# Two first weight loads on one issuing queue instead of two, in a gated MLP on one Trainium2 core

## Chip, cores, metric

One core of one Trainium2 chip. Times are device microseconds (us) of one execution. A run's profile has its own clock, which starts at 0 with the program's first instruction and covers 1.8 us less than the device time. Ratios are the mean time of one kernel's fast runs over that of the other's in the same rounds, so they are not quite the ratio of the medians that are quoted beside them.

## The reference

```python
B, S, D, F = 32, 32, 512, 1792          # bf16
gate = jnp.einsum("bsd,df->bsf", x, w1)
up   = jnp.einsum("bsd,df->bsf", x, w3)
h    = _silu(gate) * up
out  = jnp.einsum("bsf,fd->bsd", h, w2)
```

That is 1024 tokens of 512 features. In the kernel D is 4 row blocks (`dt`) of 128, F is 14 tiles (`fo`) of 128, and the tokens come in two blocks of 512.

## The kernel before

Only the start matters here. The loads, in the order of the program (SyncE is `nc.sync`, ScalarE `nc.scalar`; each has its own DMA queue, q1 and q10 in the profile):

```python
FK = 3
load_x(nc.sync, 0, 1)                              # x, token tile 0
load_x(nc.scalar, 1, 2)                            # x, token tile 1
load_w(nc.sync, w1_sb, w1_v, 0, FK, 0, 2)          # w1, tiles 0-2, row blocks 0-1
nc.scalar.activation(table[:], one, SIGMOID)
load_w(nc.scalar, w1_sb, w1_v, 0, FK, 2, DT)       # w1, tiles 0-2, row blocks 2-3
load_w(nc.sync, w3_sb, w3_v, 0, FK, 0, 2)
load_w(nc.sync, w3_sb, w3_v, 0, FK, 2, DT)
nc.sync.dma_start_transpose(out=xT[:, :, HB:NB], in_=x_flat[HB:NB, :])   # tokens 256-511
for c0, c1 in ((FK, 2 * FK), (2 * FK, 10), (10, FT)):
    load_w(nc.sync, w1_sb, w1_v, c0, c1)
    load_w(nc.sync, w3_sb, w3_v, c0, c1)
# ... transpose of tokens 512-1023, w2
```

The matmuls, in order. TensorE runs 6 dummy matmuls to raise its clock, turns tokens 0-255 with 8 matmuls (`pT`), and then:

```python
for dt in range(DT):
    for fo in range(FK):
        project(gates[fo], w1_sb, fo, 0, HB, [dt])      # gate, tokens 0-255: 12 matmuls
for dt in range(DT):
    for fo in range(FK):
        project(ups[fo], w3_sb, fo, 0, HB, [dt])        # up, tokens 0-255: 12 matmuls
for fo in range(FK):
    project(gates[fo], w1_sb, fo, HB, NB, range(DT), HB)  # tokens 256-511
    project(ups[fo], w3_sb, fo, HB, NB, range(DT), HB)
    swiglu(gates[fo], ups[fo], fo, 0)
# ... the other 11 tiles, the second block of tokens, the product with w2
```

So "w1's second half" (row blocks 2-3) is needed by the seventh gate matmul, and "the tokens" (256-511) by the twenty-fifth matmul after pT. From there on the order is fixed and TensorE hardly stops.

Of the kernel before, what the change touches and what calls it, by code (L numbers as in the profile page):

```python
# [10 lines left out]
def kernel(  # L11
# [8 lines left out]
    nc = tc.nc  # L20
# [10 lines left out]
    DT = D // P  # L31
# [7 lines left out]
    w1_v = w1.rearrange("(dt p) f -> p dt f", p=P)  # L39
# [14 lines left out]
    w1_sb = consts.tile([P, DT, F], bf16, name="w1_sb")  # L54
# [4 lines left out]
    FK = 3  # L59
# [4 lines left out]
    def load_w(queue, w_sb, w_v, c0, c1, d0=0, d1=DT):  # L64
        f0, f1 = c0 * P, c1 * P
        queue.dma_start(out=w_sb[:, d0:d1, f0:f1], in_=w_v[:, d0:d1, f0:f1])
# [5 lines left out]
    load_x(nc.scalar, 1, 2)  # L72
    load_w(nc.sync, w1_sb, w1_v, 0, FK, 0, 2)
    nc.scalar.activation(table[:], one, SIGMOID)  # L74
    load_w(nc.scalar, w1_sb, w1_v, 0, FK, 2, DT)
    load_w(nc.sync, w3_sb, w3_v, 0, FK, 0, 2)
    load_w(nc.sync, w3_sb, w3_v, 0, FK, 2, DT)
    nc.sync.dma_start_transpose(out=xT[:, :, HB:NB], in_=x_flat[HB:NB, :])
# [142 lines left out]
```

## Time and profile before

| | before |
|---|---|
| median of the first three runs (range) | 82.37 us (82.08 to 82.68) |
| span of the profile | 80.9 us |
| TensorE busy | 77.1 us (95%) |
| idle time of TensorE's weight loads put down to a load | 0.9 us for x, while the dummy matmuls still ran; 0.3 us for w1's first half |

A row of the chain of waits gives start, duration and what ran. In the timeline the bracket holds the idle time before a group and what ended it. "Landing" is the time from the start of an issue until the last of the DMA engines reports its part as written. SPq stands for SyncE issuing, PE for TensorE, L66 for line 66 of the kernel (the load in `load_w`), and "issue" for time in which nothing that the profile shows was waited for. A queue's line in a DMA view gives packets, MB, and the time that its packets took as a share of the time of the 16 DMA engines.

### The profile page before, as it was taken

The numbers are of one execution on the slowest core, as the hardware profiler recorded it, in microseconds if no ns is written. First come the engines' busy times: TensorE is split into PE (matmuls) and PEld (weight loads), VectorE is DVE, ScalarE is ACT, GpSimd is POOL, SyncE is SP. The second block draws the span as 40 slices with busy tenths as digits, with TensorE's granted clock in tenths as the row PEclk, the third lists the DMA queues.
The fourth block names the chain that finished last, engine by engine and source line by source line (L and its number), as shares of the span: only waits on it lengthen the run. The fifth ranks groups of instructions, "written<-read, shape, count | busy, mean of one in ns | idle before, by whom it ended". The sixth has DMA issues, their size and how long they took to land.

```text
span 80.9 us, 1014 instructions
## 1 busy us (share of the span) xinstructions
PE 77.1 (95%) x382; PEld 37.9 (47%) x388; DVE 39.5 (49%) x60; ACT 23.4 (29%) x40; POOL 0.7 (1%) x6
## 2 busy tenths in 40 slices
PE   6999999999999999999999999999999999999960
PEld 2368854444444444444444444444444444444540
DVE  0140399898877887877878877873000000000010
ACT  4320553222343222343222443220220220220220
POOL 3000000000000000000000000000000000000000
PEclk9999999999999999999999999999999999999999
DMA  0999999999950000000000000000011011011012
GB/s 20 291 321 281 355 351 349 171 226 330 360 193 0 0 0 0 0 0 0 4 8 0 0 0 0 4 0 0 16 49 65 26 39 65 31 42 65 28 40 62
DMA packets 10789, 7.67 MB, mean 95 GB/s; under 512 B 3616, under 2 KB 10784, under 8 KB 10784
## 3 DMA queue, kind: packets, MB, share of 16 engines
q1 hardware_dynamic: 10368, 7.28, 31.2%
q10 hardware_dynamic: 416, 0.33, 1.4%
q8 instruction: 3, 0.05, 0.2%
q14 instruction: 2, 0.02, 0.1%
HBM read 5.77 MB, written 1.05 MB: 84 GB/s over the span
## 4 chain that ended last, share of the span: by engine, by line
PE 95%; issue 1%; DVE 0%; DVEq 0%
PE gate_ps L121 31%; PE o_ps L174 30%; PE up_ps L121 30%; PE warm_ps L92 3%; PE pT L104 1%; DVE o_sb L183 0%; DVEq L183 0%
## 5 line engine op out<-in xcount | busy, mean ns | idle before, releaser
L121 PEld LDWEIGHTS <-w_sb 128*128 128x128 bf16 x248 | 24.6, 100 | 24.6 <-DMA w_sb<-in_w_dram 0.3
L121 PE MATMUL gate_ps<-xT,w_sb 128*128 128x512 bf16 (+1 forms) x122 | 29.5, 368 | 0.2
L121 PE MATMUL up_ps<-xT,w_sb 128*128 128x512 bf16 (+1 forms) x122 | 28.7, 358 | 0.1
L131 ACT ACTIVATE sig<-gate_ps 128x512 f32<-128x512 f32 x28 | 16.7, 597 | 32.3 <-PE gate_ps L121 32.3
L174 PE MATMUL o_ps<-w_sb,hT 128*128 128x512 bf16 (+2 forms) x124 | 24.3, 355 | 0.1
L133 DVE TENSOR_TENSOR t<-gate_ps,sig 128x512 f32<-128x512 f32 x28 | 19.3, 690 | 9.3 <-ACT sig L131 9.2
L134 DVE TENSOR_TENSOR hT<-t,up_ps 128x512 bf16<-128x512 f32 x28 | 19.3, 688 | 2.9
L174 PEld LDWEIGHTS <-hT 128*128 128x128 bf16 x126 | 11.8, 98 | 12.7
L183 DVE CAST o_sb<-o_ps 128x128 bf16<-128x128 f32 x1 | 0.3, 292 | 23.0 <-PE o_ps L174 23.0
L185 ACT CAST o_sb<-o_ps 128x512 bf16<-128x512 f32 (+1 forms) x8 | 4.6, 572 | 19.6 <-PE o_ps L174 19.6
L92 PE MATMUL warm_ps<-const-bfloat16-1.0 128*128 128x512 bf16 x6 | 2.7, 623 | 0.8 <-PEq L205 0.8
L114 DVE CAST xT<-pT 128x256 bf16<-128x256 f32 (+1 forms) x3 | 1.1, 380 | 3.9 <-PE pT L104 3.8
L74 ACT ACT_TABLE_LOAD x1 | 1.3, 1283 | 1.2 <-PEq L205 1.2
L92 PEld LDWEIGHTS <-const-bfloat16-1.0 128*128 128x128 bf16 x6 | 0.7, 133 | 1.9 <-issue 1.9
L104 PEld LDWEIGHTS <-x_sb 128*128 128x128 bf16 x8 | 0.8, 135 | 0.9 <-DMA x_sb<-in_x_dram 0.9
L104 PE MATMUL pT<-ident,x_sb 128*128 128x128 bf16 x8 | 1.1, 308 | 0.0
L114 ACT CAST xT<-pT 128x128 bf16<-128x128 f32 (+1 forms) x2 | 0.6, 318 | 1.5 <-PE pT L104 1.5
masks.py:199 POOL TENSOR_SCALAR_AFFINE_SELECT ident<-ident 128x128 bf16<-128x128 bf16 x1 | 0.3, 292 | 0.1
masks.py:197 POOL MEMSET ident<- 128x128 bf16 x1 | 0.2, 204 | 0.3 <-POOLq L205 0.3
L74 ACT ACTIVATE table<-const-bfloat16-1.0 128x1 f32<-128x1 bf16 x1 | 0.2, 202 | 0.0
L205 POOL MEMSET const-bfloat16-1.0<- 128x1 bf16 x1 | 0.1, 102 | 0.0
L205 POOL MEMSET const-uint8-127<- 128x1 uint8 x1 | 0.1, 102 | 0.0
(2 smaller groups left out, 0.2 us busy)
## 6 DMA issues: line engine op xcount, KB each, us to landing
w_sb<-in_w_dram SPq DMA_DIRECT2D x4, 512.0 KB, 8.0
w_sb<-in_w_dram SPq DMA_DIRECT2D x1, 1792.0 KB, 8.3
out_dram<-o_sb SPq DMA_DIRECT2D x7, 128.0 KB, 1.7
w_sb<-in_w_dram SPq DMA_DIRECT2D x2, 384.0 KB, 5.7
w_sb<-in_w_dram SPq DMA_DIRECT2D x3, 192.0 KB, 3.7
w_sb<-in_w_dram ACTq DMA_DIRECT2D x1, 192.0 KB, 3.5
x_sb<-in_x_dram ACTq DMA_DIRECT2D x1, 128.0 KB, 2.9
x_sb<-in_x_dram SPq DMA_DIRECT2D x1, 128.0 KB, 2.7
```

The source lines that it names most:

```text
L74: nc.scalar.activation(table[:], one, SIGMOID)
L92: nc.tensor.matmul(warm_ps[:, 0:cols], lhsT=one.to_broadcast([P, P]), rhs=one.to_broadcast([P, cols]), start=True, stop=True,)
L104: nc.tensor.matmul(pT[:, i, j, :], lhsT=x_sb[:, nt, dt * P : (dt + 1) * P], rhs=ident[:], start=True, stop=True,)
L114: copy(xT[:, dts[0] : dts[-1] + 1, nts[0] * P : (nts[-1] + 1) * P], pT[:].rearrange("p d t c -> p d (t c)"),)
L121: nc.tensor.matmul(ps[:, c0 : c0 + n1 - n0], lhsT=w_sb[:, dt, fo * P : (fo + 1) * P], rhs=xT[:, dt, n0:n1], start=(dt == 0), stop=(dt == D ...
L131: nc.scalar.activation(sig[:], gate_ps[:], SIGMOID)
L133: nc.vector.tensor_mul(t[:], gate_ps[:], sig[:])
L134: nc.vector.tensor_mul(hT[:, fo, nb * NB : (nb + 1) * NB], t[:], up_ps[:])
L174: nc.tensor.matmul(o_ps[:], lhsT=hT[:, fo, nt * P : (nt + 1) * P], rhs=w2_sb[:, fo, c0 : c0 + DB], start=(fo == 0), stop=(fo == FT - 1),)
L183: nc.vector.tensor_copy(o_sb[:], o_ps[:])
L185: nc.scalar.copy(o_sb[:], o_ps[:])
L205: nc = _bacc.Bacc("TRN2", target_bir_lowering=False, num_devices=1)
```

## The change

The intent was to let ScalarE issue only its half of x, so that nothing shares the DMA engines with the first half of w1, for which the first gate matmul waits.

```diff
     nc.scalar.activation(table[:], one, SIGMOID)
-    load_w(nc.scalar, w1_sb, w1_v, 0, FK, 2, DT)
+    load_w(nc.sync, w1_sb, w1_v, 0, FK, 2, DT)
     load_w(nc.sync, w3_sb, w3_v, 0, FK, 0, 2)
```

## The prediction

> **What bounds the kernel now.** I read the page's busy shares and its chain of work first, to learn which engine sets the end.
>
> ```profile
> PE 77.1 (95%) x382; PEld 37.9 (47%) x388; DVE 39.5 (49%) x60; ACT 23.4 (29%) x40; POOL 0.7 (1%) x6
> ...
> PE gate_ps L121 31%; PE o_ps L174 30%; PE up_ps L121 30%; PE warm_ps L92 3%; PE pT L104 1%; DVE o_sb L183 0%; DVEq L183 0%
> ```
>
> TensorE is busy for 77.1 of 80.9 us and nearly the whole chain is its matmuls. A change of load issues can move the end only where a matmul now waits for a load, or will wait for one. So the next view is the chain of waits in the first 11 us, in order of time.
>
> ```profile
> 0.78 2.72 PE warm_ps L92 x6
> 3.49 1.07 PE pT L104 x8
> 4.56 0.04 issue
> 4.60 2.31 PE gate_ps L121 x12
> 6.91 1.31 PE up_ps L121 x12
> ...
> 10.40 0.44 PE up_ps L121 x4
> 10.84 0.05 issue
> 10.89 0.38 PE gate_ps L121
> ```
>
> There are two pauses of 0.04 to 0.05 us and nothing else. But ends of matmuls are modelled, so I checked the joint at 4.60 us in the timeline of SyncE's and ScalarE's issues and of TensorE.
>
> ```profile
> 0.74 0.39 SPq L62 DMA_DIRECT2D x_sb<-in_x_dram  x1
> 1.20 1.44 SPq L66 DMA_DIRECT2D w_sb<-in_w_dram  x3
> 1.23 0.44 ACTq L66 DMA_DIRECT2D w_sb<-in_w_dram  x1
> 2.67 1.30 SPq L78 DMA_TRANSPOSE xT<-in_x_dram  x1
> 4.02 5.43 SPq L66 DMA_DIRECT2D w_sb<-in_w_dram  x6
> ...
> 4.60 9.42 PEld L121 LDWEIGHTS <-w_sb 128*128 128x128 bf16 x65 [0.30 <-DMA w_sb<-in_w_dram]
> ```
>
> The first gate weight load ends 0.30 us of idleness that is put down to a w1 load. The same view, cut at 4.25 us, has the last transpose matmul (pT) starting there; the eight of them start about 0.11 to 0.14 us apart, so TensorE could take the next matmul at about 4.39. The other operand, xT of row block 0, is ready earlier: VectorE's copy runs 3.79 to 4.08 and ScalarE's 3.96 to 4.23. So the path waits about 4.60 - 4.39 = **0.2 us** for the first half of w1, and this is the only wait on a load in the whole chain.
>
> **When each load lands, and when it is needed.** The issue list of the DMA view, asked for short windows, gives issue to landing for each load by itself.
>
> ```profile
> w_sb<-in_w_dram SPq DMA_DIRECT2D x1, 192.0 KB, 3.4
> w_sb<-in_w_dram ACTq DMA_DIRECT2D x1, 192.0 KB, 3.5
> ...
> w_sb<-in_w_dram SPq DMA_DIRECT2D x1, 192.0 KB, 3.8
> ...
> xT<-in_x_dram SPq DMA_TRANSPOSE x1, 4.1
> ```
>
> Added to the issue times: w1 row blocks 0-1 land at 1.20 + 3.4 = 4.6; w1 row blocks 2-3 (ScalarE) at 1.23 + 3.5 = 4.73; w3 0-1 at 1.66 + 3.7 = 5.4; w3 2-3 at 2.16 + 3.8 = 5.96; the transposed tokens 256-511 at 2.67 + 4.1 = 6.8; w1 of the second group at 4.02 + 5.4 = 9.4; w3 of it at 4.6 + 6.0 = 10.6. The timeline of the matmuls gives the needs. Gate's row block 2 is its seventh matmul, at 5.86; up starts at 6.75 and its row block 2 about 0.65 later, at 7.4; tokens 256-511 at 8.06; the second group's up at 11.54, so its gate, four matmuls of 0.216 us sooner, at about 10.7 (one of its four records is missing from the trace). Slacks are 1.1, 1.35, 1.4, 1.3, 1.3 and 0.9 us in this order, from w1's second half on.
>
> **What the Trainium skill says.** "DMA: Bandwidth & Descriptors", section "Issuing engines are not separate DMA queues": loads issued by different engines run on the same 16 DMA engines and interleave; issuing from two saves only sequencer time, "which is usually small relative to the DMA itself". The trace agrees: an issue takes 0.39 to 0.47 us against 3.4 to 3.8 to landing. The section "Queues, rings and completion order" says that each DMA engine goes round-robin between the queue rows that it has work for. The DMA view from 3 to 4 us shows that sharing between SyncE's queue (q1) and ScalarE's (q10):
>
> ```profile
> q1 hardware_dynamic: 239, 0.17, 54.6%
> q10 hardware_dynamic: 207, 0.16, 48.2%
> ```
>
> "TensorE: Matmul & The Clock Gate", Part 1, says that the array runs at half clock until an activity window of about 3.4 us, free-running, has been busy. The trace agrees on the two paces: gate matmuls of 256 columns start 0.21 us apart from 4.60 to about 6.3 us and up's start 0.11 apart, though the clock row shows full speed throughout.
>
> **The change part by part.**
>
> 1. It removes one issue of 0.44 us from ScalarE, at 1.23. ScalarE's engine is loading its table then (1.17 to 2.45) and its first copy waits for pT until 3.96. Worth 0 on the path.
>
> 2. It takes w1's second half out of competition with the first. The first half is 256 packets of 768 bytes; q1 moved 239 packets in the microsecond from 3.0, so it needed that whole microsecond beside q10. From 4.4 to 5.0, alone, q1 moved 302 packets in 0.6 us. Allowing for the slower start (67 in 0.2 us), 256 packets alone take about 0.65 us: landing at about 4.3 rather than 4.6. The gate then starts when TensorE is free, at 4.4: a gain of 0.2 us in start.
>
> 3. It puts the second half behind the first on SyncE: issue at 1.66, not 1.23. It is then in the place that w3's first half has now, with less ahead of it. All bytes up to and including it (256 KB of x, 384 KB of w1) are the same as now, and the engines are full from 3.2 us on, so I expect its data to end at about the same time, landing at 4.7 to 5.0. The need moves to 5.86 - 0.2 = 5.66. At worst, with w3's 3.7 us, it lands at 1.66 + 3.7 = 5.36, still 0.3 early. Cost 0.
>
> 4. Each later SyncE issue starts one issue (0.46 to 0.48 us) later: w3 halves at 2.14 and 2.62, the transpose at 3.15, the second group at 4.5. The w3 halves and the transpose already queue behind other data (the transpose's small packets first show at 5.0, 2.4 us after its issue began), so little of the 0.48 should reach the landings. If all of it did, the tokens would land at 7.25 (need 7.86) and the second group's w3 at 11.1 (need 11.54 - 0.2 = 11.3). Every slack remains positive. Cost 0.
>
> 5. How much of the 0.2 us survives: if the clock opens at the same moment (6.3 us), 0.2 us earlier means one more 256-column matmul at the slow pace, in place of one at 0.11, so the end comes 0.1 us sooner. If the opening moves too, 0.2. Sum: -0.1 to -0.2 us, taken as -0.12, on 82.37: **82.25 us**.
>
> **The rivals.** (a) **A new wait takes the place of the old**: SyncE's longer issue chain reaches the path at tokens 256-511 or at w3 of the second group. For it: the second has only 0.9 us of slack, of which 0.48 + 0.2 could go; in an execution whose clock opens early, TensorE arrives up to about 1 us earlier (half of 1.7 us at the slow pace) and this load becomes the bound. Against it: the DMA engines show full shares from 3.2 us on, so landings there follow bytes, not issues. It would make 82.4 to 82.8. (b) **The second half of w1 comes late**: the gate then runs six matmuls and stops at row block 2. It would need a landing after 5.66, that is 4.0 us from issue, more than any of the four small w loads took. It would make 82.5 at most. (c) **The wait is hidden anyway**: another operand (the copies of xT, or TensorE's free time) ends at 4.5 to 4.6, or the first half has the same landing since its tail is latency, not sharing. Then 82.37 stays. (d) **The clock opens in another window**: a whole window of 3.4 us at half pace is 1.7 us. It falls to both kernels alike, and the three runs of before spread over 0.6 us, so it is scatter, not an effect; yet it can move a median of few runs by 0.3.
>
> **Range and chances.** The mechanism gives 82.2 to 82.3, rival (a) up to 82.8 in the worst, and the scatter of the runs (82.08 to 82.68) is larger than the effect. I take 81.85 to 82.75. Two per cent is 1.65 us, eight times the wait that can be removed and more than any rival costs on its own: same 0.97, faster 0.01, slower 0.02.
>
> **What would show it.** Right: w1's first half lands 0.2 to 0.3 us sooner (issue to landing about 3.1), the weight load's idle time before the first gate shrinks from 0.30 to about 0.1, the first gate starts at 4.4, ScalarE's w issue is gone, the transpose is issued at about 3.15, and no other wait for a load appears before 11 us. Step 2 is wrong if the first gate still starts at 4.6 with the wait on w1; step 3 if a gap opens before the gate's seventh matmul; step 4 if one opens at tokens 256-511 or at the second group. The prediction fails if such a gap is above 0.5 us, or if the clock opens later in the changed kernel in most runs.

## The result, and the profile after

The changed kernel took 82.85 us (median of 6 runs, 82.61 to 83.02) against 82.28 us (82.08 to 82.68) before: ratio 1.0064, 95% interval 1.0036 to 1.0092. That is about 0.5 us slower, a small change but clear of the noise, and outside the predicted range.

The page's chain, by engine, shows a load on the path where there was none:

```profile
PE 89%; DMA 5%; SPq 1%; issue 1%; DVE 0%; DVEq 0%
```

The chain of waits in order of time, changed kernel:

```profile
1.20 0.42 SPq L66
1.62 0.05 issue
1.67 4.08 DMA w_sb<-in_w_dram
5.75 0.05 issue
5.79 0.83 PE gate_ps L121 x6
6.62 1.31 PE up_ps L121 x12
7.93 0.04 issue
7.97 0.60 PE gate_ps L121 x4
```

The path now runs through SyncE's second issue and through the load of w1's second half, which lands at 5.75. The timeline has the gap that this leaves:

```profile
1.20 1.96 SPq L66 DMA_DIRECT2D w_sb<-in_w_dram  x4
...
3.20 1.30 SPq L78 DMA_TRANSPOSE xT<-in_x_dram  x1
...
4.54 0.86 PE L121 MATMUL gate_ps<-xT,w_sb 128*128 128x256 bf16 x6
...
5.79 0.83 PE L121 MATMUL gate_ps<-xT,w_sb 128*128 128x256 bf16 x6 [0.39 <-DMA w_sb<-in_w_dram]
```

Six gate matmuls run, then TensorE stands until 5.79. The issue lists of w1's first half, w1's second half and the tokens:

```profile
w_sb<-in_w_dram SPq DMA_DIRECT2D x1, 192.0 KB, 3.0
...
w_sb<-in_w_dram SPq DMA_DIRECT2D x1, 192.0 KB, 4.1
...
xT<-in_x_dram SPq DMA_TRANSPOSE x1, 4.7
```

The first half lands at 1.20 + 3.0 = 4.2 (before 4.55), as the change intended. The second half lands at 5.75 (before 4.78) though its issue moved by only 0.44 us. The tokens land at 3.20 + 4.7 = 7.93 (before 6.78), 0.04 us before the matmul that uses them; going by the up matmuls' pace of 0.11 us, that matmul could have started at 7.8.

One thing in this pair of profiles misleads. The two spans, 80.9 and 80.8 us, are equal, because the clock was kinder to the changed kernel: the trace's record of full clock begins at 6.33 us in the profile before and at 4.34 us here. Before, eight gate matmuls started 0.21 us apart instead of 0.11, an estimated 0.8 us in all, which hides the loss. So more traces of both were needed before anything could be explained.

### The profile page after: what moved, and what is told of

Its sections match the earlier page's. It is cut to its first block, busy times and chain, and to the rows that moved or that the text cites. A ratio compares the mean times of both kernels' runs of the same rounds, so it can differ in the third digit from the quotient of the medians.

```text
span 80.8 us, 1014 instructions
## 1 busy us (share of the span) xinstructions
PE 76.4 (95%) x382; PEld 37.4 (46%) x388; DVE 39.4 (49%) x60; ACT 23.4 (29%) x40; POOL 0.7 (1%) x6
## 2 busy tenths in 40 slices
DMA packets 10789, 7.67 MB, mean 95 GB/s; under 512 B 3616, under 2 KB 10784, under 8 KB 10784
## 4 chain that ended last, share of the span: by engine, by line
PE 89%; DMA 5%; SPq 1%; issue 1%; DVE 0%; DVEq 0%
PE o_ps L174 30%; PE gate_ps L121 30%; PE up_ps L121 30%; DMA w_sb<-in_w_dram 5%; SPq L66 1%; SPq L62 0%; DVE o_sb L183 0%; DVEq L183 0%
## 5 line engine op out<-in xcount | busy, mean ns | idle before, releaser
L121 PEld LDWEIGHTS <-w_sb 128*128 128x128 bf16 x248 | 24.1, 98 | 24.8 <-DMA w_sb<-in_w_dram 0.9
L121 PE MATMUL gate_ps<-xT,w_sb 128*128 128x512 bf16 (+1 forms) x122 | 28.9, 358 | 0.6 <-DMA w_sb<-in_w_dram 0.4
```

The costliest lines, as they stand in the source:

```text
L121: nc.tensor.matmul(ps[:, c0 : c0 + n1 - n0], lhsT=w_sb[:, dt, fo * P : (fo + 1) * P], rhs=xT[:, dt, n0:n1], start=(dt == 0), stop=(dt == D ...
```

## The experiments

Fifteen runs were made, each timed over five rounds against the kernel before; one profile of each was kept. All gave correct results.

### Both kernels again

> The unchanged kernel once more, for a second trace and as a measure of the scatter. Theory A (the changed kernel is slower because the second half of w1, behind the first on SyncE's queue, lands 1 us later than on ScalarE's): w1's second half lands by 4.8 us and tokens 256-511 by 6.8, as in the first trace; ratio 1.000 within 0.4%. Rival R (the slow stretch in the loads from 3.5 to 5 us in the changed kernel's trace is chance and strikes either kernel): this trace can show such a stretch too, with w1 landing after 5.3 us. The clock will open somewhere between 4.3 and 7.7 us.

> The changed kernel once more. Theory A: again w1's second half lands after 5.3 us (first trace 5.75), tokens 256-511 after 7.3 (first trace 7.93), slower by 0.4 to 0.9%. Rival R: w1's second half lands at about 4.8 and the moved rate of loads stays above 300 GB/s from 3.5 to 5 us in this trace.

| | time, median (range) | ratio, 95% interval | w1 second half lands | tokens land |
|---|---|---|---|---|
| before again | 82.72 (82.17 to 84.64) | 1.0014 (0.9976 to 1.0052) | 4.76 | 7.36 |
| after again | 82.92 (82.84 to 83.29) | 1.0067 (1.0037 to 1.0096) | 6.06 | 8.17 |

(One run of before again, 84.64 us, is a slow one and is left out of the ratio.) The loss repeats, and so does the late landing; it isn't chance. For before again, theory A's 6.8 for the tokens was a miss: they landed at 7.36. That trace, whose clock record begins at 4.72, also corrects the reading of the kernel before. Its chain of waits:

```profile
2.68 4.68 DMA xT<-in_x_dram
7.36 0.04 issue
7.40 0.60 PE gate_ps L121 x4
```

Already in the kernel before, the tokens' load is on the path when the clock opens early. The first trace, with its clock opening at 6.33, was the case in which TensorE came too late to notice.

The DMA view between 3.5 and 4.75 us shows why w1's second half comes late. First the kernel before, then the changed kernel, then after again:

```profile
DMA packets 629, 0.45 MB, mean 360 GB/s; under 512 B 44, under 2 KB 629, under 8 KB 629
...
q1 hardware_dynamic: 394, 0.28, 69.6%
q10 hardware_dynamic: 235, 0.17, 40.6%
```

```profile
DMA packets 337, 0.24 MB, mean 192 GB/s; under 512 B 24, under 2 KB 337, under 8 KB 337
...
q1 hardware_dynamic: 337, 0.24, 75.2%
```

```profile
DMA packets 205, 0.15 MB, mean 119 GB/s; under 512 B 12, under 2 KB 205, under 8 KB 205
...
q1 hardware_dynamic: 205, 0.15, 60.2%
```

With ScalarE's queue (q10) empty, SyncE's queue (q1) alone moves half or a third of what the two moved before in this stretch, and the engines are partly idle. The queue has run dry, by which I mean that few packets move although its next loads have been issued. SyncE's queue thins out in the kernel before too, between w1's first half and w3, but ScalarE's queue fills the gap. The kernel before from 3.8 to 4.0 us:

```profile
q10 hardware_dynamic: 82, 0.06, 92.2%
q1 hardware_dynamic: 17, 0.01, 15.8%
```

### Is it the extra issue, or the place in the queue?

Swap w3a gives ScalarE another load in exchange, so SyncE issues as many as before.

```diff
-    load_w(nc.sync, w3_sb, w3_v, 0, FK, 0, 2)
+    load_w(nc.scalar, w3_sb, w3_v, 0, FK, 0, 2)     # on the changed kernel
```

> Both w1 halves on SyncE as in the change, but w3's first half goes to ScalarE in exchange, so SyncE issues as many loads as before and the transpose and all later loads are issued at the old times. Theory A1 (what costs is the one issue more ahead of the transpose and the second group): time as the kernel before, within 0.3%; tokens 256-511 land by 6.9. Theory A2 (what costs is w1's second half in SyncE's queue, behind the first): slower by 0.4 to 0.8%, w1's second half after 5.3.

It took 82.26 us (82.08 to 83.12), ratio 1.0006 (0.9955 to 1.0056): no loss is seen, though the interval is wide. Tokens landed at 7.15, later than A1's mark of 6.9. w1's second half landed at 5.65, later than A2's mark of 5.3, yet the engines stayed full (343 GB/s from 3.5 to 4.75), and as w1's first half was late here too (4.88, gate from 4.93), its seventh matmul stood only about 0.1 us.

Tiny issue keeps w1 as it was and only takes up an issue slot.

```diff
+    spare = consts.tile([P, 16], bf16, name="spare")    # on the kernel before
+    nc.sync.dma_start(out=spare[:], in_=x_view[:, 0, 0:16])
     load_w(nc.sync, w3_sb, w3_v, 0, FK, 0, 2)
```

> The kernel before with one more load of 4 KB on SyncE between w1's first half and w3's first half: it takes an issue slot of some 0.4 to 0.48 us and moves nearly nothing; w1's second half stays on ScalarE. Theory A1 (the shift of SyncE's later issues costs): slower by 0.3 to 0.7%, tokens 256-511 land 0.4 us or more later than in the kernel before. Theory A2: same time within 0.3%.

82.72 us, ratio 1.0035 (1.0002 to 1.0068), tokens at 7.58: 0.8 us later than in the first trace of the kernel before, 0.2 later than in the second. So this load costs something, about half of the loss by the middle of the interval, though the interval only just excludes nothing. That it is the issue slot isn't shown: the load's own small packets pass through SyncE's queue, which moved 0.19 MB from 3.5 to 4.75 us against 0.28 and 0.26 in the two traces of the kernel before.

### What makes the queue run dry?

In every trace so far SyncE was issuing the transpose at about that time (3.2 to 4.5 us in the changed kernel). Late turn moves that issue behind the second group's loads, on the changed kernel.

```diff
-    nc.sync.dma_start_transpose(out=xT[:, :, HB:NB], in_=x_flat[HB:NB, :])
     for c0, c1 in ((FK, 2 * FK), (2 * FK, 10), (10, FT)):
         load_w(nc.sync, w1_sb, w1_v, c0, c1)
         load_w(nc.sync, w3_sb, w3_v, c0, c1)
+        if c0 == FK:
+            nc.sync.dma_start_transpose(out=xT[:, :, HB:NB], in_=x_flat[HB:NB, :])
```

> The changed kernel with the transposed load of tokens 256-511 issued after the second group's loads instead of before them. In all six traces so far SyncE's queue moves little while or just after SyncE issues that transpose (3.5 to 4.75 us in the changed kernel, 3.5 to 4.0 in the kernel before, where ScalarE's queue fills in). Theory X (issuing the transpose starves SyncE's queue): w1's second half now lands by 5.0, and the stretch from 3.5 to 4.75 moves over 320 GB/s; a dry stretch may turn up near 4.2 to 5.8, when the transpose is now issued. Theory Q (one queue alone cannot feed the engines that early, whatever follows): w1's second half still lands after 5.5. The time itself gets worse, as tokens 256-511 come later: 83.5 to 85.5.

The same stretch from 3.5 to 4.75:

```profile
DMA packets 214, 0.15 MB, mean 123 GB/s; under 512 B 14, under 2 KB 214, under 8 KB 214
```

As dry as ever, with w1's second half at 6.01: theory X falls. (The time, 85.03 us, ratio 1.0315 from four fast runs, 1.0266 to 1.0365, was expected to get worse. The profiled run was a slow one, but its clock falls only at 11.12 us, long after this stretch; more of this below.)

Merged w1 puts all of w1 on SyncE in one load: one queue, but no border between two loads, and no extra issue.

```diff
-    load_w(nc.sync, w1_sb, w1_v, 0, FK, 0, 2)
+    load_w(nc.sync, w1_sb, w1_v, 0, FK)
...
-    load_w(nc.sync, w1_sb, w1_v, 0, FK, 2, DT)
```

> The changed kernel with w1's two halves in one load of 384 KB on SyncE: all of it on one queue as in the change, but as many SyncE issues as in the kernel before. Theory S (the shift of SyncE's later issues is all): tokens 256-511 land by 7.4, time as the kernel before within 0.3%. Theory Q (with ScalarE's queue empty, SyncE's queue alone leaves DMA engines idle from 3.5 to 4.75, as in after, after again and late turn): engines' share falls below 0.85 there, w1 lands after 5.2, tokens after 7.5; slower by 0.3 to 0.8%.

```profile
DMA packets 595, 0.44 MB, mean 352 GB/s; under 512 B 22, under 2 KB 595, under 8 KB 595
...
q1 hardware_dynamic: 595, 0.44, 105.2%
```

Theory Q falls as well. One queue alone fills the engines in this stretch, all of w1 is there at 4.80, and no loss is seen (82.57 us, ratio 1.0008, but a wide interval, 0.9955 to 1.0060). Theory S was off too: the tokens landed at 7.75, not by 7.4, with no extra issue ahead of them.

Hold w3 keeps SyncE from issuing anything behind w1's second half until its own part of x (token tile 0) has landed, here at 3.53.

```diff
+    nc.vector.tensor_copy(w3_sb[:, 0, 0:1], x_sb[:, 0, 0:1])   # on the changed kernel
     load_w(nc.sync, w3_sb, w3_v, 0, FK, 0, 2)
```

> The changed kernel with SyncE held back after w1's second half until x has landed (a copy of one column by VectorE, overwritten by the load, stands between): w3's loads are issued from about 3.8 on. Theory I (SyncE's further issues from 2.1 to 4.5 slow the loads already issued): w1's second half now lands by 4.9. Theory Q: it still lands after 5.3. The time itself gets worse, 83.5 to 85.

w1's second half landed at 5.06, between the two marks, and the stretch still moved only 168 GB/s; it was as thin from 3.5 to 3.74 (163 GB/s), before SyncE issued w3. So the queue runs dry without any later issue; what the later issues add to the lateness is left open. The time, 83.29 us (ratio 1.0079, 1.0024 to 1.0134), was below the expected 83.5 to 85.

That leaves the border itself. The same two loads were cut 3 and 1, and 1 and 3, instead of 2 and 2:

```diff
-    load_w(nc.sync, w1_sb, w1_v, 0, FK, 0, 2)
+    load_w(nc.sync, w1_sb, w1_v, 0, FK, 0, 3)      # split 1 and 3: 0, 1
...
-    load_w(nc.sync, w1_sb, w1_v, 0, FK, 2, DT)
+    load_w(nc.sync, w1_sb, w1_v, 0, FK, 3, DT)     # split 1 and 3: 1, DT
```

> The changed kernel with its two w1 loads on SyncE cut 3 row blocks and 1 instead of 2 and 2: same bytes, same issues. Theory L (a queue runs dry when the load ahead is used up before the next one's packets start): the first load lasts until about 3.9 us instead of 3.55, the dry stretch is shorter and shallower than in the changed kernel, the last block of w1 lands by 5.3, tokens 256-511 by 7.8; slower than before by 0.2 to 0.5%, which is what is left of the extra issue. Rival (two w1 loads behind each other disturb each other whatever the border): dry from 3.5 to 4.75 all the same, landing after 5.6; slower by 0.6% or more.

> The same cut 1 and 3. Theory L: the first load is used up at about 3.2 us, the queue is dry earlier and for longer, the three blocks land after 5.7 and the gate stands after three matmuls; slower than before by 0.6 to 1.5%. Rival (it is only the extra issue, the dry stretch costs nothing): as split 3 and 1, within 0.3% of it.

Split 3 and 1, then split 1 and 3, from 3.5 to 4.75:

```profile
DMA packets 554, 0.39 MB, mean 313 GB/s; under 512 B 44, under 2 KB 554, under 8 KB 554
```

```profile
DMA packets 265, 0.20 MB, mean 162 GB/s; under 512 B 1, under 2 KB 265, under 8 KB 265
```

Same bytes, same issues at the same times; only the border moved. With 3 blocks ahead the queue doesn't run dry, and all of w1 is there at 5.03. With 1 block ahead it is dry from 3.25 (14, 11 and 14 KB in each quarter microsecond up to 4.0, against 85 and more for a full one), the rest lands at 5.93, and between the gate's third matmul, started at 4.82, and its fourth at 5.98 TensorE stands 0.73 us. The rival of split 3 and 1 is out. The times: 82.50 us, ratio 1.0031 (0.9991 to 1.0071), and 82.82 us, ratio 1.0058 (1.0025 to 1.0090), where I had expected 0.2 to 0.5% and 0.6% or more. The first interval includes no loss at all. So the dry stretch is settled by what lies ahead of the border, but a second load's own delay doesn't explain its length. In split 3 and 1 the second load, issued at 1.67 like w1's second half in the changed kernel, moved at full rate from 3.8 to 4.1 (320 GB/s, counting the queue's bytes in the order of its loads), a time at which the changed kernel's queue was still dry (228 and 100 GB/s in its two traces). It looks as if a queue that has once run dry comes back slowly; no run tests this, and nothing here shows why.

Swap w3b is the counter-test: the two w1 halves one behind the other, and another load on ScalarE.

```diff
-    load_w(nc.sync, w3_sb, w3_v, 0, FK, 2, DT)
+    load_w(nc.scalar, w3_sb, w3_v, 0, FK, 2, DT)   # on the changed kernel
```

> Both w1 halves on SyncE, w3's second half on ScalarE: once more a load in ScalarE's queue and as many SyncE issues as before, with another load in that place than in swap w3a. Theory Q: the engines stay full from 3.0 to 5.0, w1's second half lands by 5.7 at the latest, tokens by 7.3; time as before within 0.4%. If the loss came from w1's second half being behind the first, it lands after 5.7 and the time is over by 0.5%.

355 GB/s in the stretch, w1's second half at 5.43, tokens at 6.93, 82.47 us, ratio 1.0002 (0.9952 to 1.0052). In these two swaps the second queue didn't have to hold w1; it had to hold something. As merged w1 showed, it isn't needed where w1 is one long load.

### Looking for a faster version

More scalar goes the opposite way from the change:

```diff
-    load_w(nc.sync, w3_sb, w3_v, 0, FK, 2, DT)
+    load_w(nc.scalar, w3_sb, w3_v, 0, FK, 2, DT)   # on the kernel before
```

> The opposite of the change: the kernel before with w3's second half on ScalarE as well, so SyncE issues the transpose one issue earlier, at 2.2. Theory S (what counts is how early tokens 256-511 land, as these bound the path whenever the clock opens early): they land 0.3 to 0.5 us sooner than in the kernel before (6.78 and 7.36 there), time 82.0 to 82.2, faster by 0.2 to 0.5%. Rival: no change, as the engines are full and the landing follows bytes.

A miss: 82.69 us, ratio 1.0041 (1.0001 to 1.0081). The transpose was issued 0.5 us earlier, at 2.17, and yet the tokens landed at 7.52.

Both scalar moves w1's first half to ScalarE too:

```diff
-    load_w(nc.sync, w1_sb, w1_v, 0, FK, 0, 2)
+    load_w(nc.scalar, w1_sb, w1_v, 0, FK, 0, 2)    # on the kernel before
```

> The mirror of the change: both w1 halves on ScalarE behind each other, SyncE has only w3 after its x load and one issue fewer than before. Theory S: tokens 256-511 land no later than in the kernel before (by 7.2), time 82.0 to 82.5. Theory of the place (a half behind the other on one queue lands late whatever the other queue has): w1's second half lands after 5.3.

In its trace, one of a slow run, the half left behind landed at 6.96 although SyncE had loads in flight all the while, and the tokens at 7.79; ratio 1.0089 (1.0025 to 1.0152) for its three fast runs. So behind another load on ScalarE's queue a half comes late too, as the theory of the place said; but not by the same cause, for the DMA engines had work here from 3.5 to 4.75 us (331 GB/s).

Turn scalar, on the kernel before, and after turn scalar, on the changed one, let ScalarE issue the tokens' transpose:

```diff
+    nc.scalar.dma_start_transpose(out=xT[:, :, HB:NB], in_=x_flat[HB:NB, :])   # after w1's second half
...
-    nc.sync.dma_start_transpose(out=xT[:, :, HB:NB], in_=x_flat[HB:NB, :])
```

> The kernel before with the transposed load of tokens 256-511 issued by ScalarE after w1's second half (at about 1.7) instead of by SyncE. Theory S: tokens land by 6.3 at the latest, the path is then bound by the clock and the weights alone; time 81.7 to 82.1. Theory X: SyncE's queue no longer goes dry at 3.5 to 4.0. Rival: its packets push w3's loads back and the up matmuls wait instead; time within 0.3% of before.

> The changed kernel (both w1 halves on SyncE) with that transposed load issued by ScalarE behind its x load. Theory X with S: w1's second half lands by 4.9, tokens 256-511 by 6.5, and the whole loss is gone: at or below the time of the kernel before, 81.8 to 82.4. Theory Q or a cost of w1's place in the queue: w1's second half still lands after 5.3 and the first gate pauses before its seventh matmul; slower than before by 0.3% or more.

The hoped-for gain was missed widely in both: 84.20 us (ratio 1.0217, 1.0168 to 1.0266, so unclear at 2%), and 85.93 us with only one fast run (83.32). The transpose, issued at 1.7 or 1.2, still landed only at 8.56 and 7.80, and the weights issued around it came late: w3's second half at 8.84 in the one, w1's second half at 7.68 in the other (the trace of a slow run). That is what the rival of the first and the second theory of the other had named, though at a greater cost. That the transpose's packets held the weights up is likely, but not tested by itself.

Merged both has w1 and w3 of the first group in one load each on SyncE (the diff is that of merged w1, done for w3 as well).

> w1 and w3 of the first group in one load each, both on SyncE: two issues fewer than in the kernel before, the transpose issued at about 2.2, and no short load that can run out before the next starts. Theory L with S: w1 lands by 4.9, w3 by 6.1, tokens 256-511 by 7.2; time 81.9 to 82.4, up to 0.6% faster than before. Rival: w3 comes whole and so too late for the first up matmuls (needed at 6.2 when the clock opens early); same or slower.

A miss: 82.94 us, ratio 1.0065 (1.0025 to 1.0105). The gate now waits for all of w1, until 4.91, and the tokens landed at 7.69, although their issue came at 2.20. No version beat the kernel before.

### What sets the time

The traces of all fast runs (late turn, both scalar and after turn scalar were profiled in a slow one). "None" is a trace that holds no such record; the pace of the matmuls there changes at about 5 us or before (in split 1 and 3, whose gate stood, between 4.82 and 5.98).

| trace | clock record begins | tokens land | first gate matmul of tokens 256-511 | time of that run |
|---|---|---|---|---|
| before | 6.33 | 6.78 | 8.06 | 82.69 |
| before again | 4.72 | 7.36 | 7.40 | 82.17 |
| swap w3b | 4.70 | 6.93 | 7.45 | 82.11 |
| tiny issue | 5.22 | 7.58 | 7.63 | 82.46 |
| swap w3a | none | 7.15 | 7.67 | 82.34 |
| more scalar | 5.40 | 7.52 | 7.73 | 82.36 |
| merged w1 | 3.66 | 7.75 | 7.79 | 82.50 |
| split 3 and 1 | none | 7.78 | 7.82 | 82.46 |
| after | 4.34 | 7.93 | 7.97 | 82.61 |
| after again | none | 8.17 | 8.21 | 82.85 |
| split 1 and 3 | none | 8.02 | 8.28 | 82.91 |
| merged both | 6.79 | 7.69 | 8.44 | 83.20 |
| hold w3 | 6.72 | 9.18 | 9.22 | 83.86 |
| turn scalar | 4.78 | 8.56 | 9.55 | 84.18 |

The last column less the one before it is 74.6 to 74.8 us in every row. So the whole difference between these runs is made before that matmul. It starts either 0.04 to 0.05 us after the tokens land (before again, tiny issue, merged w1, split 3 and 1, after, after again, hold w3), or when TensorE is through with the 24 matmuls ahead of it, which depends on when its clock opens and on how long it stood for a weight load. In both traces of the changed kernel it is the tokens: after the gap for w1's second half TensorE could have gone on at 7.77 and 8.08 (its last up matmul and 0.11 us), so the gap alone would have cost up to 0.2 us less.

When the tokens land has a second cause, which the experiments didn't test. The DMA view from 5.75 to 6.5 us, when the transpose's small packets move, for before, before again and merged w1:

```profile
DMA packets 616, 0.20 MB, mean 270 GB/s; under 512 B 513, under 2 KB 616, under 8 KB 616
DMA packets 429, 0.11 MB, mean 150 GB/s; under 512 B 424, under 2 KB 429, under 8 KB 429
DMA packets 143, 0.04 MB, mean 59 GB/s; under 512 B 127, under 2 KB 143, under 8 KB 143
```

The queue runs thin a second time, in one trace of the kernel before and not in the other. Before and swap w3b, with the earliest tokens (6.78 and 6.93), moved 270 and 266 GB/s; before again, more scalar, tiny issue, merged w1 and split 3 and 1, with tokens at 7.36 to 7.78, moved 150, 156, 179, 59 and 116. Swap w3a (210, tokens at 7.15) and merged both (198, 7.69) lie between. In the changed kernel's two traces it was not this (232 and 307): there the loss came in the first dry stretch. Why the second one comes is open, and it remains a rival to the extra issue as the reason why the tokens are late in tiny issue and in split 3 and 1.

## Why the prediction was wrong

- **Step 1** (nothing lost or won on ScalarE): nothing in the traces speaks against it.
- **Step 2** was right in its mechanism. w1's first half landed at 4.20 and 4.04, predicted 4.3; the gate started at 4.54 and 4.32, predicted 4.4. The gain in start was under the 0.2 us that was forecast, 0.06 and 0.13 (from 4.60 and 4.45): in the first trace x landed later, at 3.67 against 3.42, and in before again there was hardly a wait to remove, as the last pT matmul started at 4.31.
- **Step 3 failed.** It argued from bytes: the same bytes ahead, full engines, so the same end, "landing at 4.7 to 5.0", at worst 5.36. Measured were 5.75 and 6.06, after the need at 5.66. The engines didn't stay full: 192 and 119 GB/s where the kernel before had 360. That they had been full was itself an effect of the second queue. The view that I had shown for "sharing" (q1 54.6%, q10 48.2% from 3 to 4 us) I read as a cost of sharing alone; it was also cover. Rival (b), which I had dismissed because no small load had ever taken 4.0 us, came true with 4.1 and 4.4, though its time, 82.5 at most, was passed, because the tokens came late as well.
- **Step 4 failed** in its reading of slack. The 1.3 us for the tokens came from one trace, whose clock happened to open late. In before again there was no slack at all: TensorE was ready at 7.19 instead of 8.06, and the tokens landed at 7.36 instead of 6.78. I had named the early clock under rival (a), but worked it into the slack of w3 only, and not into that of the tokens. Their landing moved from 6.78 and 7.36 to 7.93 and 8.17, where the step had 7.25 as its worst.
- **Step 5's sum** of -0.1 to -0.2 us therefore became about +0.5 us. Rival (a), at 82.4 to 82.8, was nearest, and 0.05 us short of the median. (That two per cent is more than any rival costs is a slip: rival (d) has 1.7 us against 1.65. Nothing hangs on it.)
- **The parts of the loss.** With an extra issue and a shallow dry stretch or none, 0.31 and 0.35% were measured (split 3 and 1, not clear of zero; tiny issue); the change costs 0.64 and 0.67%. How the loss divides between the issue and the dry stretch is not shown: the intervals are wide, the second thin stretch is in both of these traces, and more scalar, with an issue fewer ahead of the tokens, lost 0.41%. With a load back on ScalarE and no extra issue (swap w3a, swap w3b), no loss is seen, within half a per cent.
- **What would show it**: the signs listed for steps 3 and 4, a gap before the gate's seventh matmul and one at tokens 256-511, are those that appeared.
- **Left open**: why the queue thins out at the border of two loads and takes about a microsecond to come back, how much of the second half's lateness the later issues add, and what makes the second thin stretch.

## What to carry to other kernels

A slack read from one profile holds for that execution; where TensorE's clock opens at a different time in each, take several traces, or work out each slack for the earliest clock. Equal bytes land at equal times only while the DMA engines have something to do: in the first 5 us of this kernel either one long load or a second queue with work kept them full at the border behind a short load. Look whether yours are. Before taking work from a queue that looks idle, ask what it was covering.

## What the Trainium skill lacked or had wrong

- "DMA: Bandwidth & Descriptors", section "Issuing engines are not separate DMA queues", says that issuing from several engines only saves the sequencer's time. Here a load of 192 KB in the second queue was also what kept the engines full between 3.5 and 4.75 us: 343 to 360 GB/s with it, 119 and 192 GB/s without (kernel before and both swaps against the changed kernel's two traces). With w1 as one load, one queue did it too (352 GB/s).
- That page doesn't describe a queue that thins out at the border of two loads of which the second has long been issued. Measured: with 96 or 192 KB of w1 ahead of the border, 162 and 119 to 192 GB/s from 3.5 to 4.75 us; with 288 KB ahead or with no border, 313 and 352 GB/s.
- "TensorE: Matmul & The Clock Gate", Part 1, gives the moment of warming as about 4 us into sustained matmuls, give or take 0.5 us, and says elsewhere that it varies from run to run. The clock records of these traces begin at 3.53 to 6.79 us, that is 2.8 to 6.0 us after the first matmul, always at about 0.77: a spread of 3.3 us, worth an estimated 1.6 us at half pace.
- The same page, section "Why this matters for your kernels", advises against pauses of TensorE above some 3 us. Here shorter ones were sometimes followed by the loss of the clock; that the pause caused it isn't tested. In late turn a pause from 7.92 to 10.38 (2.5 us) was followed by 3.4 us of half clock, in both scalar the half clock began within one from 5.39 to 7.01 (1.6 us). In turn scalar a pause from 6.86 to 8.88 (2.0 us) had no such loss. (Times are from start to start of the matmuls around the pause.) The second and third stretch of late turn, TensorE alone (busy, clock, DMA share, GB/s):

```profile
11.20:14.40 3.20, 3.20 (x17) 0.50 1.09 347
14.60:17.80 3.20, 3.20 (x17) 1.00 1.24 172
```

